# Loading the K cache in 4 MB transfers of 32 KB rows, and stepping attention over pairs of units

## The chip, the cores and the metric

The kernel runs on one core of a Trainium2 chip. The metric is the device time of one execution in microseconds (us), lower being better. A run also has a span, from the first to the last instruction of the profile, which is about 1.9 us shorter. A single-core run is called fast or slow by its distance from the fastest run of the same kernel; where a kernel ran once, its state is unknown. Each profile gives the TensorE clock that was granted (1.00 is full speed).

## The reference

A decode step (one token for each of two batch entries): a layer norm, attention over the last 2048 of 8192 cached positions, and an MLP with a squared ReLU, all added to the input. Everything is bf16.

```python
# B=2, Sq=1, D=576, 32 query heads on 16 K/V heads, Dh=128, window W=2048, F=4608
xn = layernorm(x)
q = xn @ wq                                         # wq: 576 x 4096
k, v = k_cache[:, :, Sk - W:], v_cache[:, :, Sk - W:]   # [2, 16, 2048, 128] each
p = softmax(q k^T * Dh**-0.5)
attn = (p v) @ wo                                   # wo: 4096 x 576
h = relu(xn @ w1 + b1) ** 2                         # w1: 576 x 4608
return x + attn + h @ w2 + b2                       # w2: 4608 x 576
```

Each of K and V has 16.8 MB in the window, the four weight matrices 20 MB together: 53.6 MB to bring in, and very little arithmetic on each byte.

## The kernel before

The work is cut into 8 units, each of four K/V heads of one batch entry. A unit's K (2 MB) lies in SBUF with 128 partitions = 32 chunks of positions x 4 heads, and each partition holds one row of 16 KB (64 positions x 128 x 2 bytes). V lies in the same way.

```python
TH = 4; CP = P // TH            # 4 heads, 32 chunks
NJ = W // CP                    # 64 positions in a row
UE = NJ * Dh                    # 8192 elements, 16 KB
kvpool = ctx.enter_context(tc.tile_pool(name="kvpool", bufs=6))   # 6 slots for K, V and w2

def unit_view(cache, u):
    tq, b = divmod(u, B)
    return cache[b, tq * TH:(tq + 1) * TH, S0:Sk, :].rearrange("h (c j) d -> c h (j d)", c=CP)
```

TensorE transposes K (two bf16 as one f32), ACT and DVE take turns in evicting 128x1024 from PSUM, and eight matmuls make half of a unit's scores. The softmax and the product with V (called PV here) follow one and two units later. `sc_ps`, `pv_ps` and `kT_ps` are the PSUM tiles of these steps.

```python
dst = kT[:, gw * PG:(gw + 1) * PG, :, :].rearrange("p i s e -> p (i s e)")   # contiguous
...
pe_mm(sc_ps[32 * k:32 * (k + 1), :, :], lhsT=qz[...], rhs=kT[:, e, :, 32 * k:32 * (k + 1)], ...)
...
def step(u, p=None, o=None):       # unit u: K transposes and scores; softmax of u-1; PV of p = u-2
    transposes(u, 0); softmax_max(u - 1); transposes(u, 1); softmax_exp(u - 1) ...
# ... (cut) the order of the large transfers on one queue:
# k0 wq k1 v0 w1 k2 v1 k3 v2 k4 v3 k5 v4 k6 v5 wo0 k7 v6 v7 wo1 w2
```

Of the kernel before, what the change touches and what calls it, by code (L numbers as in the profile page):

```python
# [8 lines left out]
F32 = mybir.dt.float32  # L9
# [7 lines left out]
def kernel(  # L17
# [14 lines left out]
    nc = tc.nc  # L32
# [14 lines left out]
    NC = TH * rep  # L47
    NQ = Hkv // TH
    NU = NQ * B
    JG = 8  # L50
    NG = NJ // JG
    NT = NJ // 4
    PG = JG // 2
    GW = NT // PG
    UE = NJ * Dh

    HP = 2 * D // P
# [14 lines left out]
    BIG = 1e30  # L72

    const = ctx.enter_context(tc.tile_pool(name="const", bufs=1))
    kvpool = ctx.enter_context(tc.tile_pool(name="kvpool", bufs=6))
    ktpool = ctx.enter_context(tc.tile_pool(name="ktpool", bufs=2))
    wbig = ctx.enter_context(tc.tile_pool(name="wbig", bufs=1))
    work = ctx.enter_context(tc.tile_pool(name="work", bufs=2))
    keep = ctx.enter_context(tc.tile_pool(name="keep", bufs=3))
# [2 lines left out]
    def pe_mm(out, **kw):  # L82
        return tc.keep_in_program_order(nc.tensor.matmul(out, **kw))  # L83
# [9 lines left out]

    k_tiles, v_tiles, w_tiles, wo_tiles, w2_tiles = {}, {}, {}, {}, {}

    def unit_view(cache, u):
        tq, b = divmod(u, B)
        return cache[b, tq * TH:(tq + 1) * TH, S0:Sk, :].rearrange("h (c j) d -> c h (j d)", c=CP)

    def issue_kv(tiles, cache, u, name, parts=1):  # L100
        tl = kvpool.tile([P, UE], BF16, tag="kv", name=f"{name}_{u}")
        v = unit_view(cache, u)
        n = UE // parts
        tiles[u] = tl
        return [lambda i=i: nc.sync.dma_start(out=tl[:, i * n:(i + 1) * n], in_=v[:, :, i * n:(i + 1) * n])  # L105
                for i in range(parts)]

    def issue_w(wt, name, width):
        tl = wbig.tile([P, HP * FL], BF16, tag="wbig", name=f"{name}_sb")
        nc.sync.dma_start(out=tl[:, 0:HP * width], in_=wt.rearrange("d (s l) -> (d s) l", s=2)  # L110
                          .rearrange("(p r) l -> p (r l)", r=HP))
        w_tiles[name] = tl

    def issue_wo(t):
        if t == 0:
            wo_tiles["all"] = wbig.tile([P, B * WR, D], BF16, tag="wbig", name="wo_sb")
        tl = wo_tiles["all"][:, t * WR:(t + 1) * WR, :]
        n = P * WR
        nc.sync.dma_start(out=tl, in_=A_wo[t * n:(t + 1) * n, :].rearrange("(p r) n -> p r n", r=WR))
        wo_tiles[t] = tl  # L120

    w2_rows = {}

    def issue_w2(g, r0, r1):
        if r0 == 0:
            w2_rows[g] = kvpool.tile([P, FR * D], BF16, tag="kv", name=f"w2_{g}")
        tl = w2_rows[g][:, r0 * D:r1 * D]
        rows = B_w2[g * HW:(g + 1) * HW, :].rearrange("(p r) n -> p (r n)", r=FR)
        nc.sync.dma_start(out=tl, in_=rows[:, r0 * D:r1 * D])
        w2_tiles[(g, r0)] = tl  # L130
# [1 line left out]
    x_sb = const.tile([B + 1, D], BF16, name="x_sb")  # L132
    nc.scalar.dma_start(out=x_sb[0:B, :], in_=x2d)
    b1_sb = const.tile([NG4, HW], BF16, name="b1_sb")
    for g in range(2):
        nc.scalar.dma_start(out=b1_sb[2 * g:2 * g + 2, :], in_=B_b1[2 * g * HW:2 * (g + 1) * HW].rearrange("(g n) -> g n", g=2))
    for i in range(2):
        nc.scalar.dma_start(out=x_sb[B:B + 1, i * OH:(i + 1) * OH],
                            in_=B_b2[i * OH:(i + 1) * OH].rearrange("(o n) -> o n", o=1))
    eps_t = const.tile([B, 1], F32, name="eps_t")  # L140
    nc.vector.memset(eps_t[:], 1e-5)
    warm = const.tile([B, 122], F32, name="warm")
    nc.scalar.activation(out=warm[:, 0:1], in_=eps_t[:], func=ACT.Sqrt)
    for f in issue_kv(k_tiles, A_k_cache, 0, "k"):
        f()
    issue_w(A_wq, "wq", QL)
    ones_f = work.tile([P, P], F32, tag="mix0", name="ones_f")
    nc.vector.memset(ones_f[:], 1.0)
# [118 lines left out]

    kT_tiles, sc_tiles, pT_tiles, acc_tiles, sm_tiles = {}, {}, {}, {}, {}

    def transposes(u, g):  # L270
        k_sb = k_tiles[u]
        w, gw = divmod(g, GW)
        if gw == 0:
            kT_tiles[(u, w)] = ktpool.tile([P, NT, P, 2], BF16, tag="kT_sb", name=f"kT_{u}_{w}")
        kT = kT_tiles[(u, w)]
        kT_ps = psum.tile([P, PG, P], F32, tag="kT", bufs=3, name=f"kT_ps_{u}_{g}")
        for i in range(PG):
            q = g * PG + i
            pe_tr(out=kT_ps[:, i, :], in_=k_sb[:, 2 * q * Dh:2 * (q + 1) * Dh].bitcast(F32),
                                identity=ident_f[:])  # L280
        src = kT_ps[:].rearrange("p i s -> p (i s)").bitcast(BF16)
        dst = kT[:, gw * PG:(gw + 1) * PG, :, :].rearrange("p i s e -> p (i s e)")
        if g % 2 == 0:
            pin(nc.scalar.copy(out=dst, in_=src))  # L284
        else:
            pin(nc.vector.tensor_copy(out=dst, in_=src))  # L286

    def scores(u, w):
        tq, b = divmod(u, B)
        if w == 0:  # L290
            sc_tiles[u] = psum.tile([P, NT, 32], F32, tag="sc", bufs=2, name=f"sc_ps_{u}")
            pe_mm(sc_tiles[u][:].rearrange("p t s -> p (t s)"), lhsT=qhead[:], rhs=khead[:],
                             start=True, stop=False, skip_group_check=True)
        sc_ps = sc_tiles[u]
        kT = kT_tiles.pop((u, w))[:].rearrange("p t s e -> p e t s")
        for e in range(2):
            for k in range(4):
                pe_mm(sc_ps[32 * k:32 * (k + 1), :, :],
                                      lhsT=qz[:, e, b * NQ + tq, w, :, :].rearrange("p j c -> p (j c)"),
                                      rhs=kT[:, e, :, 32 * k:32 * (k + 1)], start=False, stop=(w == 1 and e == 1),  # L300
                                      skip_group_check=True, tile_position=(0, 32 * k))

    sm_cur = {}
# [1 line left out]
    def softmax_max(u):  # L305
        sc_ps = sc_tiles.pop(u)[:].rearrange("p t s -> p (t s)")
        mx = work.tile([P, 1], F32, tag="mx", name=f"mx_{u}")
        pin(nc.vector.tensor_reduce(out=mx[:], in_=sc_ps, axis=AX.X, op=ALU.max))  # L308
        m2 = work.tile([P, NC], F32, tag="m2", name=f"m2_{u}")
        pin(nc.vector.tensor_scalar(out=m2[:], in0=offm[:], scalar1=mx[:, 0:1], scalar2=None, op0=ALU.add))  # L310
        gmax = work.tile([P, NC], F32, tag="gmax", name=f"gmax_{u}")
        nc.gpsimd.partition_all_reduce(gmax[:], m2[:], channels=P, reduce_op=ReduceOp.max)  # L312
        sm_cur[u] = (sc_ps, gmax)
# [20 lines left out]
    def pv_start(u):  # L334
        pv_cur[u] = psum.tile([P, 4, Dh], F32, tag="misc", name=f"pv_ps_{u}")
# [28 lines left out]
    wo_state = {}  # L364

    def pv_out(u):
        tq, b = divmod(u, B)
        t, half = divmod(tq, 2)
        if u % (2 * B) == 0:
            sm_tiles[t] = psum.tile([P, B, Dh + 1], F32, tag="sm", name=f"sm_{t}")  # L370
# [80 lines left out]
                                 rhs=w2_sb[:, o + i * OQ:o + (i + 1) * OQ], start=False, stop=(r == FR - 1),  # L451
                                 skip_group_check=True, tile_position=(0, 32 * i))

    def load_k(u):
        for f in issue_kv(k_tiles, A_k_cache, u, "k"):
            f()

    def load_v(u):
        for f in issue_kv(v_tiles, A_v_cache, u, "v"):
            f()  # L460

    W2P = [(0, 0, 9), (1, 0, 9), (2, 0, 9), (3, 0, 7), (3, 7, 9)]

    load_k(1)
    load_v(0)
    issue_w(B_w1, "w1", FL)
    load_k(2)
    load_v(1)
    load_k(3)

    NR = NT // 4

# [3 lines left out]
            pv(u, i)  # L476
        pv_mix(u)

    def step(u, p=None, o=None):
        if p is not None:  # L480
            pv_start(p)
        transposes(u, 0)
        softmax_max(u - 1)
        transposes(u, 1)
        softmax_exp(u - 1)
        transposes(u, 2)
        if p is not None:
            pv(p, 0)
        transposes(u, 3)
        if p is not None:  # L490
            pv(p, 1)
        softmax_tr(u - 1)
        if o is not None:
            pv_out(o)
        transposes(u, 4)
        scores(u, 0)
        for g in range(GW + 1, NG):
            transposes(u, g)
        for i in range(2, NR):
# [12 lines left out]
    step(1)
    pv_all(0)
    mlp_h_start()
    mlp_h_all()
    mlp_h_end()
    load_k(4)
    for u in range(2, NU - 1):
        step(u, u - 2 if u > 2 else None, u - 3 if u > 2 else None)
        if u == 2:  # L520
            out_acc(res_b[:], lambda a, z: x_sb[:, a:z], start=True)
        if u + 1 < NU - 1:
            load_v(u + 1)
        if u == 4:
            issue_wo(0)
        if u + 3 < NU:
            load_k(u + 3)
        if u == 5:
            load_v(NU - 1)
    issue_wo(1)  # L530
    for w in W2P:
        issue_w2(*w)
    step(NU - 1, NU - 3, NU - 4)
    pv_start(NU - 2)
    for i in range(NR):
        pv(NU - 2, i)
    softmax_max(NU - 1)
    pv_out(NU - 3)
    softmax_exp(NU - 1)
    pv_mix(NU - 2)  # L540
    softmax_tr(NU - 1)
    pv_out(NU - 2)
    pv_all(NU - 1)
    wo_acc(0)
    pv_out(NU - 1)
    mlp_o(*W2P[0])
    wo_acc(1)
# [47 lines left out]
```

## Time and profile before

| | before |
|---|---|
| time | 134.14 us median of 4 runs (133.96 to 134.19) |
| span of the profiled run | 132.2 us, granted clock 0.884 |
| bytes read | 53.62 MB |
| busy of PE, DVE, ACT | 89.0, 59.1, 44.2 us |
| mean packet of 16 KB (2048 of them) | 0.616 us, 426 GB/s over 16 engines |
| idle of the 16 DMA engines, from span start to last packet | 3.0 us, of which 2.1 before the first |

The prediction below shows the main lines of this profile.

 "Packets" here are the trace's records of single DMA moves; on the large loads there is one for each row, and a mean packet time means their mean.

### The profile page before, as it was taken

The numbers are of one execution on the slowest core, as the hardware profiler recorded it, in microseconds if no ns is written. First come the engines' busy times: TensorE is split into PE (matmuls) and PEld (weight loads), VectorE is DVE, ScalarE is ACT, GpSimd is POOL, SyncE is SP. The second block draws the span as 40 slices with busy tenths as digits, with TensorE's granted clock in tenths as the row PEclk, the third lists the DMA queues.
The fourth block names the chain that finished last, engine by engine and source line by source line (L and its number), as shares of the span: only waits on it lengthen the run. The fifth ranks groups of instructions, "written<-read, shape, count | busy, mean of one in ns | idle before, by whom it ended". The sixth has DMA issues, their size and how long they took to land.

```text
span 132.2 us, 2040 instructions
## 1 busy us (share of the span) xinstructions
PE 89.0 (67%) x830; PEld 54.7 (41%) x830; DVE 59.1 (45%) x150; ACT 44.2 (33%) x64; POOL 7.7 (6%) x26
## 2 busy tenths in 40 slices
PE   0069319789862967879889389789303996399761
PEld 0059202639521354744466064466003661155540
DVE  6944400224640019246675823778800358644011
ACT  2705401015700226438457145357100751200011
POOL 7700000001000001000010000010000000000000
PEclk9999995955999599689999977999985699959999
DMA  4999989999998999999999999999999999999950
GB/s 154 389 451 479 413 382 431 431 484 477 439 404 350 436 416 441 426 446 416 431 431 426 436 421 439 426 429 431 428 441 416 446 423 422 429 420 433 419 238 1
DMA packets 3632, 53.74 MB, mean 406 GB/s; under 512 B 412, under 2 KB 420, under 8 KB 680
## 3 DMA queue, kind: packets, MB, share of 16 engines
q1 hardware_dynamic: 3604, 53.61, 95.2%
q8 instruction: 6, 0.10, 0.3%
q10 hardware_dynamic: 20, 0.01, 0.0%
q14 instruction: 2, 0.02, 0.0%
HBM read 53.62 MB, written 0.00 MB: 405 GB/s over the span
## 4 chain that ended last, share of the span: by engine, by line
DMA 72%; PE 20%; DVE 2%; ACT 2%; issue 1%; SPq 1%; DVEq 0%; ACTq 0%
DMA k<-in_A_k_cache_dram 44%; DMA w<-in_B_w_dram 14%; DMA wq_sb<-in_A_wq_dram 13%; PE kT_ps L86 10%; PE sc_ps L83 4%; PE q_ps L83 3%; PE pv_ps L83 2%; PE qs_ps L83 1%; DVE kT L286 1%; ACT kT L284 1%; ACT pr L323 1%; PE sm L83 1%; DVE qrow L250 1%; SPq L105 0%; DVE qz L266 0%
## 5 line engine op out<-in xcount | busy, mean ns | idle before, releaser
L86 PE MATMUL kT_ps<-ident_f,k 128*128 128x128 f32 x256 | 41.4, 319 | 12.6 <-DMA k<-in_A_k_cache_dram 12.1
L284 ACT COPY kT<-kT_ps 128x1024 bf16<-128x1024 bf16 x32 | 31.9, 1011 | 36.8 <-PE kT_ps L86 34.0
L86 PEld LDWEIGHTS kT_ps<-ident_f,k 128*128 128x128 f32 x256 | 34.4, 165 | 21.9 <-issue 16.6
L286 DVE COPY kT<-kT_ps 128x1024 bf16<-128x1024 bf16 x32 | 22.1, 691 | 31.9 <-PE kT_ps L86 31.8
L83 PE MATMUL sc_ps<-kT,qz 128*32 128x512 bf16 x128 | 10.7, 418 | 4.5 <-DVE kT L286 2.8
L83 PE MATMUL pv_ps<-v,pT 128*32 128x512 bf16 x128 | 11.7, 435 | 1.0 <-DVE acc L358 0.8
L312 POOL PARTITION_ALL_REDUCE gmax<-m x8 | 2.9, 365 | 103.1 <-DVE m L310 103.1
L323 ACT ACTIVATE pr<-sc_ps,nb 128x512 bf16<-128x512 f32 x8 | 5.5, 687 | 7.9 <-DVE nb L320 7.9
L83 PEld LDWEIGHTS <-xnT 128*4 128x4 bf16 x90 | 2.9, 105 | 11.6 <-issue 11.0
L308 DVE TENSOR_REDUCE mx<-sc_ps 128x1 f32<-128x512 f32 x8 | 5.5, 683 | 3.1 <-PE sc_ps L83 3.1
L83 PE MATMUL q_ps<-wq_sb,xnT 128*4 128x512 bf16 x36 | 3.7, 592 | 4.5 <-DMA wq_sb<-in_A_wq_dram 4.5
L83 PEld LDWEIGHTS <-qz 128*32 128x32 bf16 x128 | 2.3, 98 | 10.1 <-DVE kT L286 6.3
L83 PE MATMUL h_ps<-w_sb,xnT 128*4 128x384 bf16 x54 | 3.9, 420 | 3.4 <-DMA w_sb<-in_B_w_dram 3.4
L358 DVE SCALAR_TENSOR_TENSOR mix<-pv_ps,own_j,mix 128x128 f32<-128x128 f32 x16 | 5.6, 352 | 0.6
L329 DVE STREAM_TRANSPOSE pT<-pr 128x512 bf16<-128x512 bf16 x8 | 5.6, 702 | 0.2 <-ACT pr L323 0.2
L86 PE MATMUL pro_ps<-ident,xs 2*128 2x2 bf16 x10 | 0.6, 164 | 7.6 <-DVE xs L180 7.6
L83 PE MATMUL out_ps<-wo_sb,ws 128*2 128x288 bf16 x64 | 5.1, 323 | 0.3 <-DVE ws L387 0.3
L83 PEld LDWEIGHTS <-pT 128*32 128x32 bf16 x128 | 2.9, 98 | 5.9 <-issue 3.5
L551 ACT COPY part<-out_ps 2x288 f32<-2x288 f32 x1 | 0.4, 389 | 13.5 <-PE out_ps L83 13.5
L83 PE MATMUL sm<-acc,tohead 128*64 128x129 f32 x16 | 3.7, 313 | 1.8 <-DVE acc L358 1.8
L431 DVE TENSOR_TENSOR hs<-hT_ps,hodd 128x20 f32<-128x20 f32 (+1 forms) x4 | 0.5, 172 | 9.2 <-ACT hodd L428 9.2
L83 PE MATMUL out_ps<-w,hT_sb 128*2 128x288 bf16 x54 | 3.8, 286 | 1.1 <-DMA w<-in_B_w_dram 1.1
(78 smaller groups left out, 58.2 us busy)
## 6 DMA issues: line engine op xcount, KB each, us to landing
k<-in_A_k_cache_dram SPq DMA_DIRECT2D x8, 2048.0 KB, 7.7
v<-in_A_v_cache_dram SPq DMA_DIRECT2D x8, 2048.0 KB, 16.9
w_sb<-in_B_w_dram SPq DMA_DIRECT2D x1, 5184.0 KB, 19.3
wq_sb<-in_A_wq_dram SPq DMA_DIRECT2D x1, 4608.0 KB
wo_sb<-in_A_wo_dram SPq DMA_DIRECT2D x2, 2304.0 KB
w<-in_B_w_dram SPq DMA_DIRECT2D x3, 1296.0 KB, 27.2
w<-in_B_w_dram SPq DMA_DIRECT2D x1, 1008.0 KB
w<-in_B_w_dram SPq DMA_DIRECT2D x1, 288.0 KB
```

What stands on the lines that cost most here:

```text
L83: return tc.keep_in_program_order(nc.tensor.matmul(out, **kw))
L86: return tc.keep_in_program_order(nc.tensor.transpose(**kw))
L250: nc.vector.tensor_copy(out=qrow[:, 0, :], in_=q_ps[0][0:RB, :])
L284: pin(nc.scalar.copy(out=dst, in_=src))
L286: pin(nc.vector.tensor_copy(out=dst, in_=src))
L308: pin(nc.vector.tensor_reduce(out=mx[:], in_=sc_ps, axis=AX.X, op=ALU.max))
L312: nc.gpsimd.partition_all_reduce(gmax[:], m2[:], channels=P, reduce_op=ReduceOp.max)
L323: pin(nc.scalar.activation(out=pr[:], in_=sc_ps, func=ACT.Exp, bias=nb[:], scale=scale, accum_out=acc[:, Dh:Dh + 1]))
L329: pin(nc.vector.transpose(out=pT[:].rearrange("p t m -> p (t m)"), in_=pr[:]))
L358: op = nc.vector.scalar_tensor_tensor(out=nx, in0=pv_ps[:, j, :], scalar=own_j[:, j:j + 1], in1=acc, op0=ALU.mult, op1=ALU.add)
L431: nc.vector.tensor_tensor(out=hs[:].rearrange("p (g r) b -> p r g b", g=NG4)[:, r0:r0 + n, g:g + 2, :], in0=even[:, :, g:g + 2, :], in1=od ...
L551: cp(out=part[:, i * OH:(i + 1) * OH], in_=out_ps[32 * i:32 * i + B, :])
```

## The change

Its intent: half as many K transfers, of rows twice as long. Two units (a pair) share one 4 MB K tile, whose 128 partitions are 16 chunks x 8 heads with 32 KB rows. The transposed K then holds the two units' heads side by side, so evictions write runs of 16 elements and the scores read every second group of four. SBUF for 4 MB tiles is found by giving V three slots, and by putting odd K pairs where wq and w1 had been. So the second K pair now waits for the product with w1, and the loop steps over pairs: 8 slices of transposes for both units, then scores of both, with two softmaxes and two PVs in between.

```diff
-    kvpool = ctx.enter_context(tc.tile_pool(name="kvpool", bufs=6))
+    kvpool = ctx.enter_context(tc.tile_pool(name="kvpool", bufs=3))
+    kpool = ctx.enter_context(tc.tile_pool(name="kpool", bufs=1))
+    wopool = ctx.enter_context(tc.tile_pool(name="wopool", bufs=1))
...
+    def load_k(pr):                      # K2 = 8 heads, C2 = 16 chunks
+        t, b = divmod(pr, B)
+        if pr % 2 == 0:
+            tl = kpool.tile([P, 2 * UE], BF16, tag="kA", name=f"k_{pr}")
+        else:
+            tl = wbig.tile([P, 2 * UE], BF16, tag="wbig", name=f"k_{pr}")
+        nc.sync.dma_start(out=tl[:], in_=A_k_cache[b, t * K2:(t + 1) * K2, S0:Sk, :]
+                          .rearrange("h (c j) d -> c h (j d)", c=C2))
+        k_tiles[pr] = tl
...
-        dst = kT[:, gw * PG:(gw + 1) * PG, :, :].rearrange("p i s e -> p (i s e)")
+        dst = kT[:, gw * PG:(gw + 1) * PG, :, a, :, :].rearrange("p i c h e -> p (i c) (h e)")
...
-                                      rhs=kT[:, e, :, 32 * k:32 * (k + 1)], start=False, stop=(w == 1 and e == 1),
+                                      rhs=kT[:, e, :, nb * k:nb * (k + 1), q * TH:(q + 1) * TH],
...
+    issue_w(B_w1, "w1", FL)
+    load_v(2)
...                                       # softmax, PV of units 0 and 1; the MLP's first product
     mlp_h_end()
-    load_k(4)
-    for u in range(2, NU - 1):
-        step(u, u - 2 if u > 2 else None, u - 3 if u > 2 else None)
...
+    load_k(1)
+    load_v(3)
+    load_k(2)
+    load_v(4)
+    pair(1)
+    load_k(3)
+    pair(2, None, 2, (more_v5, lambda: load_v(6)))
+    pair(3, 3, 4, (lambda: load_v(7), lambda: None), lambda: wo_acc(0))
```

More of the change, by code (lines that the diff above doesn't have):

```diff
@@ L49 @@
     NU = NQ * B
-    JG = 8
-    NG = NJ // JG
+    NP = NU // 2
+    K2 = 2 * TH
+    C2 = P // K2
     NT = NJ // 4
-    PG = JG // 2
+    PG = 4
     GW = NT // PG
+    NG = 4 * GW
     UE = NJ * Dh
@@ L94, with unit, load_v @@
     k_tiles, v_tiles, w_tiles, wo_tiles, w2_tiles = {}, {}, {}, {}, {}
-    def unit_view(cache, u):
-        tq, b = divmod(u, B)
-        return cache[b, tq * TH:(tq + 1) * TH, S0:Sk, :].rearrange("h (c j) d -> c h (j d)", c=CP)
-    def issue_kv(tiles, cache, u, name, parts=1):
-        tl = kvpool.tile([P, UE], BF16, tag="kv", name=f"{name}_{u}")
-        v = unit_view(cache, u)
-        n = UE // parts
-        tiles[u] = tl
-        return [lambda i=i: nc.sync.dma_start(out=tl[:, i * n:(i + 1) * n], in_=v[:, :, i * n:(i + 1) * n])
-                for i in range(parts)]
+    def unit(u):
+        pr, q = divmod(u, 2)
+        t, b = divmod(pr, B)
+        return 2 * t + q, b
+    def load_k(pr):
+        t, b = divmod(pr, B)
+        if pr % 2 == 0:
[5 more added lines that the diff above has]
+        k_tiles[pr] = tl
+    def load_v(u):
+        tq, b = unit(u)
+        tl = kvpool.tile([P, UE], BF16, tag="v", name=f"v_{u}")
+        nc.sync.dma_start(out=tl[:], in_=A_v_cache[b, tq * TH:(tq + 1) * TH, S0:Sk, :]
+                          .rearrange("h (c j) d -> c h (j d)", c=CP))
+        v_tiles[u] = tl
     def issue_w(wt, name, width):
@@ L114, in issue_wo @@
     def issue_wo(t):
-        if t == 0:
-            wo_tiles["all"] = wbig.tile([P, B * WR, D], BF16, tag="wbig", name="wo_sb")
-        tl = wo_tiles["all"][:, t * WR:(t + 1) * WR, :]
+        tl = wopool.tile([P, WR, D], BF16, tag="wo_sb", name=f"wo_{t}")
         n = P * WR
-        nc.sync.dma_start(out=tl, in_=A_wo[t * n:(t + 1) * n, :].rearrange("(p r) n -> p r n", r=WR))
+        nc.sync.dma_start(out=tl[:], in_=A_wo[t * n:(t + 1) * n, :].rearrange("(p r) n -> p r n", r=WR))
         wo_tiles[t] = tl
@@ L124, in issue_w2 @@
     def issue_w2(g, r0, r1):
-        if r0 == 0:
-            w2_rows[g] = kvpool.tile([P, FR * D], BF16, tag="kv", name=f"w2_{g}")
-        tl = w2_rows[g][:, r0 * D:r1 * D]
+        if g == 0:
+            w2_rows["all"] = kpool.tile([P, (NG4 - 1) * FR * D], BF16, tag="kA", name="w2_rows")
+        if g == NG4 - 1 and r0 == 0:
+            w2_rows[g] = kvpool.tile([P, FR * D], BF16, tag="v", name=f"w2_{g}")
+        o = g * FR * D
+        tl = w2_rows["all"][:, o:o + FR * D] if g < NG4 - 1 else w2_rows[g][:, r0 * D:r1 * D]
         rows = B_w2[g * HW:(g + 1) * HW, :].rearrange("(p r) n -> p (r n)", r=FR)
@@ L134 @@
     b1_sb = const.tile([NG4, HW], BF16, name="b1_sb")
-    for g in range(2):
-        nc.scalar.dma_start(out=b1_sb[2 * g:2 * g + 2, :], in_=B_b1[2 * g * HW:2 * (g + 1) * HW].rearrange("(g n) -> g n", g=2))
-    for i in range(2):
-        nc.scalar.dma_start(out=x_sb[B:B + 1, i * OH:(i + 1) * OH],
-                            in_=B_b2[i * OH:(i + 1) * OH].rearrange("(o n) -> o n", o=1))
     eps_t = const.tile([B, 1], F32, name="eps_t")
@@ L143 @@
     nc.scalar.activation(out=warm[:, 0:1], in_=eps_t[:], func=ACT.Sqrt)
-    for f in issue_kv(k_tiles, A_k_cache, 0, "k"):
-        f()
+    load_k(0)
     issue_w(A_wq, "wq", QL)
@@ L268, with transposes @@
     kT_tiles, sc_tiles, pT_tiles, acc_tiles, sm_tiles = {}, {}, {}, {}, {}
-    def transposes(u, g):
-        k_sb = k_tiles[u]
-        w, gw = divmod(g, GW)
-        if gw == 0:
-            kT_tiles[(u, w)] = ktpool.tile([P, NT, P, 2], BF16, tag="kT_sb", name=f"kT_{u}_{w}")
-        kT = kT_tiles[(u, w)]
-        kT_ps = psum.tile([P, PG, P], F32, tag="kT", bufs=3, name=f"kT_ps_{u}_{g}")
+    def transposes(pr, g):
+        k_sb = k_tiles[pr]
+        w, gw = divmod(g, 2 * GW)
+        a, gw = divmod(gw, GW)
+        if a == 0 and gw == 0:
+            kT_tiles[(pr, w)] = ktpool.tile([P, NT, C2, 2, K2, 2], BF16, tag="kT_sb", name=f"kT_{pr}_{w}")
+        kT = kT_tiles[(pr, w)]
+        kT_ps = psum.tile([P, PG, P], F32, tag="kT", bufs=3, name=f"kT_ps_{pr}_{g}")
         for i in range(PG):
-            q = g * PG + i
+            q = (a * 2 + w) * NT + gw * PG + i
             pe_tr(out=kT_ps[:, i, :], in_=k_sb[:, 2 * q * Dh:2 * (q + 1) * Dh].bitcast(F32),
                                 identity=ident_f[:])
-        src = kT_ps[:].rearrange("p i s -> p (i s)").bitcast(BF16)
-        dst = kT[:, gw * PG:(gw + 1) * PG, :, :].rearrange("p i s e -> p (i s e)")
+        src = kT_ps[:].rearrange("p i s -> p (i s)").bitcast(BF16).rearrange("p (n x) -> p n x", x=2 * K2)
+        dst = kT[:, gw * PG:(gw + 1) * PG, :, a, :, :].rearrange("p i c h e -> p (i c) (h e)")
         if g % 2 == 0:
@@ L288, in scores @@
     def scores(u, w):
-        tq, b = divmod(u, B)
+        tq, b = unit(u)
+        pr, q = divmod(u, 2)
         if w == 0:
@@ L294, in scores @@
         sc_ps = sc_tiles[u]
-        kT = kT_tiles.pop((u, w))[:].rearrange("p t s e -> p e t s")
+        kT = kT_tiles[(pr, w)][:].rearrange("p t c a h e -> p e t (c a) h")
+        nb = 32 // TH
         for e in range(2):
             for k in range(4):
-                pe_mm(sc_ps[32 * k:32 * (k + 1), :, :],
+                pe_mm(sc_ps[32 * k:32 * (k + 1), :, :].rearrange("m t (n h) -> m t n h", h=TH),
                                       lhsT=qz[:, e, b * NQ + tq, w, :, :].rearrange("p j c -> p (j c)"),
-                                      rhs=kT[:, e, :, 32 * k:32 * (k + 1)], start=False, stop=(w == 1 and e == 1),
+                                      rhs=kT[:, e, :, nb * k:nb * (k + 1), q * TH:(q + 1) * TH],
+                                      start=False, stop=(w == 1 and e == 1),
                                       skip_group_check=True, tile_position=(0, 32 * k))
@@ L366, in pv_out @@
     def pv_out(u):
-        tq, b = divmod(u, B)
+        tq, b = unit(u)
         t, half = divmod(tq, 2)
@@ L452, in mlp_tail @@
                                  skip_group_check=True, tile_position=(0, 32 * i))
-    def load_k(u):
-        for f in issue_kv(k_tiles, A_k_cache, u, "k"):
-            f()
-    def load_v(u):
-        for f in issue_kv(v_tiles, A_v_cache, u, "v"):
-            f()
     W2P = [(0, 0, 9), (1, 0, 9), (2, 0, 9), (3, 0, 7), (3, 7, 9)]
-    load_k(1)
     load_v(0)
-    issue_w(B_w1, "w1", FL)
-    load_k(2)
     load_v(1)
-    load_k(3)
     NR = NT // 4
@@ L477, in pv_all, with pair @@
         pv_mix(u)
-    def step(u, p=None, o=None):
-        if p is not None:
-            pv_start(p)
-        transposes(u, 0)
-        softmax_max(u - 1)
-        transposes(u, 1)
-        softmax_exp(u - 1)
-        transposes(u, 2)
-        if p is not None:
-            pv(p, 0)
-        transposes(u, 3)
-        if p is not None:
-            pv(p, 1)
-        softmax_tr(u - 1)
-        if o is not None:
-            pv_out(o)
-        transposes(u, 4)
-        scores(u, 0)
-        for g in range(GW + 1, NG):
-            transposes(u, g)
-        for i in range(2, NR):
-            if p is not None:
-                pv(p, i)
-        if p is not None:
-            pv_mix(p)
-        scores(u, 1)
+    def pair(pr, o=None, p0=None, after=(), mid=None):
+        p1 = p0 + 1 if p0 is not None else None
+        u0, u1 = 2 * pr, 2 * pr + 1
+        if p0 is not None:
+            pv_start(p0)
+        for g in range(2 * GW):
+            transposes(pr, g)
+            if p0 is None:
+                continue
+            if g == 0:
+                softmax_max(p0)
+            if g == 1:
+                softmax_exp(p0)
+            if g == 2:
+                softmax_max(p1)
+            if g == 3:
+                softmax_tr(p0)
+                softmax_exp(p1)
+                if o is not None:
+                    pv_out(o)
+            if g == 5:
+                softmax_tr(p1)
+                pv(p0, 0)
+                pv(p0, 1)
+        if p0 is not None:
+            pv(p0, 2)
+        scores(u0, 0)
+        if p0 is not None:
+            pv(p0, 3)
+            pv_mix(p0)
+            after[0]()
+        scores(u1, 0)
+        if mid is not None:
+            mid()
+        for g in range(2 * GW, NG):
+            transposes(pr, g)
+            if p0 is None:
+                continue
+            if g == 2 * GW + 1:
+                pv_out(p0)
+                pv_start(p1)
+                pv(p1, 0)
+            if g == 2 * GW + 4:
+                pv(p1, 1)
+        if p0 is not None:
+            pv(p1, 2)
+            pv(p1, 3)
+            pv_mix(p1)
+            after[1]()
+        scores(u0, 1)
+        scores(u1, 1)
     for g in range(NG):
@@ L508 @@
     q_all()
-    for w in range(2):
-        scores(0, w)
-    load_v(2)
-    step(1)
+    issue_w(B_w1, "w1", FL)
+    load_v(2)
+    b1_sb = const.tile([NG4, HW], BF16, name="b1_sb")
+    nc.gpsimd.dma_start(out=b1_sb[:], in_=B_b1.rearrange("(g n) -> g n", g=NG4))
+    nc.gpsimd.dma_start(out=x_sb[B:B + 1, :], in_=B_b2.rearrange("(o n) -> o n", o=1))
+    for w in range(2):
+        for u in range(2):
+            scores(u, w)
+    for u in range(2):
+        softmax_max(u)
+        softmax_exp(u)
+        softmax_tr(u)
     pv_all(0)
+    pv_out(0)
+    pv_all(1)
     mlp_h_start()
@@ L516, with more_v5 @@
     mlp_h_end()
-    load_k(4)
-    for u in range(2, NU - 1):
-        step(u, u - 2 if u > 2 else None, u - 3 if u > 2 else None)
-        if u == 2:
-            out_acc(res_b[:], lambda a, z: x_sb[:, a:z], start=True)
-        if u + 1 < NU - 1:
-            load_v(u + 1)
-        if u == 4:
-            issue_wo(0)
-        if u + 3 < NU:
-            load_k(u + 3)
-        if u == 5:
-            load_v(NU - 1)
+    pv_out(1)
+    load_k(1)
[3 more added lines that the diff above has]
+    pair(1)
+    out_acc(res_b[:], lambda a, z: x_sb[:, a:z], start=True)
+    load_k(3)
+    def more_v5():
+        load_v(5)
+        issue_wo(0)
+    pair(2, None, 2, (more_v5, lambda: load_v(6)))
+    pair(3, 3, 4, (lambda: load_v(7), lambda: None), lambda: wo_acc(0))
     issue_wo(1)
@@ L532 @@
         issue_w2(*w)
-    step(NU - 1, NU - 3, NU - 4)
     pv_start(NU - 2)
+    softmax_max(NU - 2)
+    softmax_max(NU - 1)
+    pv_out(NU - 3)
+    softmax_exp(NU - 2)
+    softmax_tr(NU - 2)
     for i in range(NR):
         pv(NU - 2, i)
-    softmax_max(NU - 1)
-    pv_out(NU - 3)
     softmax_exp(NU - 1)
+    softmax_tr(NU - 1)
     pv_mix(NU - 2)
-    softmax_tr(NU - 1)
     pv_out(NU - 2)
     pv_all(NU - 1)
-    wo_acc(0)
     pv_out(NU - 1)
```

## The prediction

116.6 us to the last scores, 22.9 of tail and 1.9 beyond the span come to its 141.5 us. What went is an argument that longer rows have little to win, the reason for keeping 691 ns for the new eviction (so it stands as an assumption; 690 was measured), and the third rival, slower evictions or scores, whose size rested on a figure not shown. The "cold start" stands on the trace: 12 transposes took 2.79 us after 7.54 us idle, with a granted clock of 0.50 from 101 to 104 us, and 1.50 us after 0.76, with 1.00 from 66 to 69.

> **What bounds the kernel now.** I read the page of the profile first: the slices of the span, the DMA queues, and the shares of the chain that ended last.
>
> ```profile
> DMA  4999989999998999999999999999999999999950
> q1 hardware_dynamic: 3604, 53.61, 95.2%
> DMA 72%; PE 20%; DVE 2%; ACT 2%; issue 1%; SPq 1%; DVEq 0%; ACTq 0%
> ```
>
> The DMA row is busy in nearly every slice, the main queue's packets fill 95.2% of 16 engines' span, and 72% of the chain is DMA. So the kernel waits for bytes: 53.61 MB / (0.952 x 132.2 us) = 426 GB/s while the engines work. The packet records of the trace show the first large packet at 2.1 us, the last one ending at 128.65 us, and under 0.5 us of idle engine time between 4 and 126 us. The program then needs 3.6 us more. Nothing of the stream's middle can be won by better overlap.
>
> Next I asked the table of engine busy time by stage, because a reordering of transfers moves work between stages (columns: stretch, length, busy of PE, weight loads, DVE, ACT, POOL, clock, DMA share, GB/s).
>
> ```profile
> 24.00:53.00 29.00, 21.34 (x187) 13.92 (x187) 10.28 (x28) 9.10 (x17) 0.73 (x2) 0.82 1.01 431
> 53.00:66.00 13.00, 11.49 (x97) 7.01 (x96) 6.80 (x15) 6.85 (x9) 0.36 (x1) 0.87 1.00 429
> 66.00:101.00 35.00, 23.05 (x201) 13.45 (x201) 19.88 (x47) 14.06 (x18) 1.46 (x4) 0.91 1.01 431
> ```
>
> TensorE is far from idle: it works in every stage, with one 2 MB K slice per unit arriving steadily, and it has only modest slack. That slack is what the change spends. The TensorE timeline gives the cost of one unit (columns: start, duration, engine, line, operation, idle before).
>
> ```profile
> 66.58 1.50 PE L86 MATMUL kT_ps<-ident_f,k 128*128 128x128 f32 x12 [0.76 <-DMA k<-in_A_k_cache_dram]
> ...
> 73.40 0.62 PE L83 MATMUL sc_ps<-kT,qz 128*32 128x512 bf16 x8 [0.24 <-DVE kT L286]
> ...
> 101.43 2.79 PE L86 MATMUL kT_ps<-ident_f,k 128*128 128x128 f32 x12 [7.54 <-DMA k<-in_A_k_cache_dram]
> ```
>
> A full unit (32 transposes, their evictions, scores, softmax of the previous unit, PV of an earlier one) takes 66.58 to 74.0 = 7.4 us. The transfers of a unit (K and V, 2 x 4.93 us) take 9.9 us. Unit 5 starts at its K's landing; the last unit starts at 101.43, and after its scores (110.4) the program needs 21.8 us more. The evictions that pace the transposes are:
>
> ```profile
> L284 ACT COPY kT<-kT_ps 128x1024 bf16<-128x1024 bf16 x32 | 31.9, 1011 | 36.8 <-PE kT_ps L86 34.0
> L286 DVE COPY kT<-kT_ps 128x1024 bf16<-128x1024 bf16 x32 | 22.1, 691 | 31.9 <-PE kT_ps L86 31.8
> ```
>
> [...] 12 transposes took 2.79 us after 7.54 us idle and 1.50 us after 0.76. [...] I keep 691 ns.
>
> **The change part by part.**
>
> *Longer K rows.* Mean packet times by row size in the trace: 0.616 us for 16 KB, 0.686 for 18,432 bytes, 1.365 for 36,864, 1.542 for 41,472. That is 426 to 432 GB/s. A 32 KB row should take 1.22 us instead of 2 x 0.616 = 1.23. Each engine carries 32 such rows: about 0.4 us saved in all. No byte is removed.
>
> *Order of the transfers.* Before, the queue ran k0, wq, k1, v0, w1, k2, v1, k3, v2, k4. After, the order of instructions on the issuing queue is k0 (4 MB), wq, v0, v1, w1, v2, v3, then k1 (4 MB), k2, v4, k3, v5, wo0, v6, v7, wo1, w2. Pair 1 (units 2 and 3) can't start before k1 lands. In units of 8 packets per engine: k0 9.73 + wq 10.92 + v0, v1 9.86 + w1 12.34 + v2, v3 9.86 + k1 9.73 = 62.4 us. Added to the start at 2.1 us this gives 64.5. The same sum for the fifth K before gives 64.8, against a first transpose at 66.58, so I add 1.7: pair 1 starts at about 66.3 us.
>
> This is the point of the prediction. Before, at 66.6 us TensorE had finished units 0 to 4 and had three to go. After, at 66.3 it has done units 0 and 1 and has six to go, having stood idle since w1's product (about 46 to 53 us). The transfers left then last only 60 us.
>
> *TensorE's work after 66.3 us.* Pair 1 carries no PV: 16 groups at about 0.6 us (1.0 us of ACT and 0.69 of DVE alternate over three PSUM buffers) and four scores of 0.55 to 0.85, waits for the last eviction included: 13.0 us, plus 1.5 us for its cold start. Pair 2 carries PV of two units and two softmaxes: 2 x 7.4 = 14.8 plus 2 us, because both exponentials and both probability transposes stand between its first eight evictions: 16.9. Pair 3 the same plus one output projection of 2.0 (32 matmuls, 121.62 to 123.58 before): 18.9. Sum: 66.3 + 1.5 + 13.0 + 16.9 + 18.9 = 116.6 for the end of the last scores, against 110.4 before.
>
> *The tail.* Now the softmax of both last units comes after the last scores. First PV of the tail: rest of the mixes 0.7, two maxima of 0.92, 0.4 for the bias, exponential 0.95, transpose 0.75, some waits: 5 us (0.8 before). Then 4 us to the second PV (111.22 to 115.06 before), 4.8 us for it, its mixes, the first w2 part and the normalisation, 2.0 + 2.4 for the second projection and two w2 parts, 2.5 for part, tail and cast, 2.1 to the end of the span: 22.9 us with rounding. Span 116.6 + 22.9 = 139.5. The profiled run before took 134.06 for a span of 132.2, so I add 1.9: **141.5 us**.
>
> *Buffers.* Three V slots: v5 waits for PV of unit 2 and v7 for PV of unit 4, each in the middle of a pair. v7 is due at about 105 on the queue and its slot comes free at about 107: a gap of 2 to 3 us in the stream, perhaps 1 us at v5 or k3. Last w2 landing then 130 to 132 us, still ahead of TensorE's use, so the gap is not added.
>
> **The rivals.** (1) *Stream still the bound*: if pairs run as fast as pure TensorE time (10.5 + 13.6 + 15.6 instead of 48.8 us), the last scores end at 107 and the stream decides: 134.2 - 0.4 plus 0 to 2 us of slot gaps, 134 to 136 us. For it: DMA busy at 95%. Against it: evictions and softmax already held a unit to 7.4 us, with 6.8 of TensorE work. (2) *Gain*: even with the stream perfect and the tail kept, the floor is 2.1 + 125.2 + 3.6 + 1.9 = 132.8 us, 1% faster. Over 2% faster would need a DMA rate that no row size here shows. [...]
>
> **Range and chances.** TensorE's chain is summed over 70 us with 10% doubt on waits and clock: 137.5 to 146.5. Under 2% change needs rival 1. Faster 0.02, same 0.12, slower 0.86.
>
> **What would show it.** First transposes of pair 1 at 66 us with over 10 us of TensorE idle before, waiting for K; then no more K waits: k2 and k3 landed before TensorE asks. Chain with much less DMA, far more PE, DVE and ACT. Evictions near 1011 and 691 ns; K packets near 1.22 us. Last scores at 114 to 119 us. A wait of the queue for PV before v7, with a dip in the DMA row. If pair 1 starts well before 66 us, or pairs take under 12, 15 and 17 us, I am wrong.

## More of the kernel before

```profile
GB/s 154 389 451 479 413 382 431 431 484 477 439 404 350 436 416 441 426 446 416 431 431 426 436 421 439 426 429 431 428 441 416 446 423 422 429 420 433 419 238 1
...
k<-in_A_k_cache_dram SPq DMA_DIRECT2D x8, 2048.0 KB, 7.7
```

The rate lies near 430 GB/s whatever large load is in flight: by their mean packets, 426 to 432 GB/s for rows of 10,368 to 41,472 bytes.

## The result

The changed kernel takes **180.96 us** (median of 4 runs; 178.69 and 178.84 in the fast, 183.08 and 183.96 in the slow). The ratio to before is 1.333, 95% interval 1.330 to 1.336. A ratio is the mean time of one kernel's fast runs over that of the other's of the same rounds, so it is not quite the ratio of the medians quoted. The prediction had the direction right and the size wrong: 141.5 us, range 137.5 to 146.5.

The profiled run after (span 177.0 us, clock 0.774) in the same views. First its page: the DMA row and the rate in 40 slices, the main queue (packets, MB, share of 16 engines), the chain that ended last, the evictions (count | busy, mean ns | idle before), and K's transfers.

```profile
DMA  7899999899999999999899979999899999999930
GB/s 186 170 239 237 235 416 400 370 441 414 450 452 411 433 370 230 237 215 192 185 237 237 215 218 370 244 222 207 170 218 426 405 437 437 428 413 433 418 123 1
...
q1 hardware_dynamic: 3028, 53.61, 94.7%
...
DMA 58%; PE 27%; DVE 9%; ACT 3%; issue 1%; ACTq 0%; DVEq 0%
...
L294 ACT COPY kT<-kT_ps 128x1024 bf16<-128x1024 bf16 x32 | 31.7, 1012 | 78.5 <-PE kT_ps L90 78.5
L296 DVE COPY kT<-kT_ps 128x1024 bf16<-128x1024 bf16 x32 | 22.1, 690 | 75.3 <-PE kT_ps L90 75.3
...
k<-in_A_k_cache_dram SPq DMA_DIRECT2D x4, 4096.0 KB, 32.5
```

By the DMA row and the queue's share of 94.7% (95.2% before), the engines are as busy as before, although the kernel is a third slower and moves the same 53.61 MB. **Busy is not moving.** The rate row shows it: 170 to 244 GB/s in slices 1 to 5, 16 to 24 and 26 to 30 (counted from 1), and 370 to 452 in the others until the stream ends. The table by stage takes three stretches (stretch, length, busy of PE, weight loads, DVE, ACT, POOL, granted clock, DMA share, GB/s): by the order of the queue, the first and third hold K alone, the second w1 and V.

```profile
2.00:22.00 20.00, 0.57 (x10) 0.41 (x10) 5.83 (x22) 3.85 (x6) 4.54 (x14) 1.00 1.05 232
36.00:55.00 19.00, 10.44 (x86) 4.18 (x86) 6.49 (x18) 3.73 (x8) 0.73 (x2) 0.58 1.01 431
66.00:88.00 22.00, 0.00 (x0) 0.00 (x0) 0.00 (x0) 0.00 (x0) 0.00 (x0) 0.50 1.03 216
```

From 66 to 88 us no compute engine does anything, and the DMA share is full at half the rate. In the packet records, 512 rows of 32 KB took a mean of **2.448 us** (median 2.51), which is 214 GB/s over 16 engines; before, a 16 KB row took 0.616. All other sizes are nearly as they were: means of 0.687 for 18,432 bytes, 1.410 for 36,864 and 1.538 for 41,472, and a median of 0.611 us for V's 16 KB (mean 0.657; 0.616 before). So the change made the loads of K, and only these, run at half their rate. TensorE's timeline shows what it paid (start, duration, instructions, idle before and its releaser):

```profile
88.59 6.26 PE L90 MATMUL kT_ps<-ident_f,k 128*128 128x128 f32 x32 [23.38 <-DMA k<-in_A_k_cache_dram]
...
107.55 3.90 PE L90 MATMUL kT_ps<-ident_f,k 128*128 128x128 f32 x20 [3.76 <-DMA k<-in_A_k_cache_dram]
...
134.35 3.65 PE L90 MATMUL kT_ps<-ident_f,k 128*128 128x128 f32 x16 [10.19 <-DMA k<-in_A_k_cache_dram]
```

All three remaining pairs wait for their K, where the prediction had one such wait, for pair 1 alone at 66.3 us.

### The profile page after: what moved, and what is told of

The parts are those of the page before. It is cut to its first block, busy times and chain, and to the rows that moved or that the text cites. A ratio compares the mean times of both kernels' runs of the same rounds, so it can differ in the third digit from the quotient of the medians.

```text
span 177.0 us, 2015 instructions
## 1 busy us (share of the span) xinstructions
PE 92.5 (52%) x830; PEld 57.3 (32%) x830; DVE 59.3 (33%) x150; ACT 47.0 (27%) x66; POOL 8.9 (5%) x28
## 3 DMA queue, kind: packets, MB, share of 16 engines
q1 hardware_dynamic: 3028, 53.61, 94.7%
## 4 chain that ended last, share of the span: by engine, by line
DMA 58%; PE 27%; DVE 9%; ACT 3%; issue 1%; ACTq 0%; DVEq 0%
DMA k<-in_A_k_cache_dram 46%; PE kT_ps L90 13%; DMA w_sb<-in_B_w_dram 12%; PE out_ps L87 5%; PE h_ps L87 3%; ACT kT L294 2%; DVE kT L296 2%; PE sc_ps L87 2%; PE pv_ps L87 2%; DVE pT L342 2%; DVE mix L371 1%; PE q_ps L87 1%; DVE mx L321 1%; PE sm L87 1%; ACT pr L336 1%
## 5 line engine op out<-in xcount | busy, mean ns | idle before, releaser
L90 PEld LDWEIGHTS kT_ps<-ident_f,k 128*128 128x128 f32 x256 | 35.8, 169 | 60.5 <-issue 40.8
L294 ACT COPY kT<-kT_ps 128x1024 bf16<-128x1024 bf16 x32 | 31.7, 1012 | 78.5 <-PE kT_ps L90 78.5
L87 PE MATMUL pv_ps<-v,pT 128*32 128x512 bf16 x128 | 12.4, 475 | 7.2 <-DVE pT L342 4.0
L325 POOL PARTITION_ALL_REDUCE gmax<-m x8 | 2.9, 366 | 146.5 <-DVE m L323 146.0
L87 PE MATMUL sm<-acc,tohead 128*64 128x129 f32 x16 | 4.4, 369 | 7.3 <-DVE acc L371 7.3
L87 PEld LDWEIGHTS sm<-acc,tohead 128*64 128x64 f32 x16 | 1.9, 171 | 10.9 <-issue 10.1
L368 DVE TENSOR_SCALAR mix<-pv_ps,own_j 128x128 f32<-128x128 f32 x8 | 2.7, 338 | 7.8 <-PE pv_ps L87 7.8
L87 PE MATMUL h_ps<-w_sb,xnT 128*4 128x384 bf16 x54 | 5.0, 521 | 0.1
L87 PE MATMUL out_ps<-wo,ws 128*2 128x288 bf16 x64 | 4.8, 307 | 0.0
L87 PE MATMUL out_ps<-w_rows,hT_sb 128*2 128x288 bf16 x54 | 4.7, 338 | 0.0
## 6 DMA issues: line engine op xcount, KB each, us to landing
w<-in_B_w_dram SPq DMA_DIRECT2D x1, 1008.0 KB, 18.9
```

The source lines that it names most:

```text
L87: return tc.keep_in_program_order(nc.tensor.matmul(out, **kw))
L90: return tc.keep_in_program_order(nc.tensor.transpose(**kw))
L294: pin(nc.scalar.copy(out=dst, in_=src))
L325: nc.gpsimd.partition_all_reduce(gmax[:], m2[:], channels=P, reduce_op=ReduceOp.max)
L368: op = nc.vector.tensor_scalar(out=nx, in0=pv_ps[:, j, :], scalar1=own_j[:, j:j + 1], scalar2=None, op0=ALU.mult)
```

## The experiments

Four theories were open. *Length* (A): rows of 32 KB are slow in themselves. *Memory* (B): the memory side is slow, with eight heads read at once, each at a distance of 2 MB. *Form* (C): the transfer is slow because its source of 16 chunks x 8 rows is spread over the DMA engines, or over the partitions, in some bad way. *Order*: K's rate is only a part, and the new order of steps costs much too. Thirteen kernels ran. Those that read K at another place, or put it into another order, are called wrong. The comparison with the reference for these inputs does not notice which part of K was read, so that it proves nothing there, and little about K in the kernels marked correct. Runs of the kernel before, made beside them, took 134.04 to 134.59 us. For each, the table by stage shows the same stretch, 3 to 11 us, in which only the first K loads.

### k16_32x4: the change with K as before

Each pair's K is loaded as two 2 MB transfers of 16 KB rows, with 4 heads x 32 chunks; the transposed K is laid out for each unit on its own. Order, pools and pairs stay changed. 3 rounds, correct.

```diff
-        nc.sync.dma_start(out=tl[:], in_=A_k_cache[b, t * K2:(t + 1) * K2, S0:Sk, :]
-                          .rearrange("h (c j) d -> c h (j d)", c=C2))
+        for q in range(2):
+            h = (2 * t + q) * TH
+            nc.sync.dma_start(out=tl[:, q * UE:(q + 1) * UE], in_=A_k_cache[b, h:h + TH, S0:Sk, :]
+                              .rearrange("h (c j) d -> c h (j d)", c=CP))
```

> The changed kernel with its queue order, slots and pairs, but each 4 MB of K loaded as two transfers of 16 KB rows from 4 heads by 32 chunks, as before; correct result. All three theories of the slow K (A: rows of 32 KB are slow in themselves; B: eight heads 2 MB apart collide in HBM; C: the 16 by 8 shape [...]) expect K packets of 0.62 us here. The prediction's own chain of TensorE work after the late second K pair then expects 141.5 us (137.5 to 146.5), and the slow K costs the rest, about 37 us. If the order costs nothing: 134 us.

138.98 us (137.58 to 139.21), ratio to before 1.033 (1.028 to 1.038). The mean 16 KB packet is back at 0.625 us. Its table by stage, and its chain:

```profile
3.00:11.00 8.00, 3.25 (x23) 3.09 (x24) 5.60 (x19) 3.87 (x5) 3.53 (x12) 1.00 1.00 421
```

```profile
PE 46%; DMA 26%; DVE 15%; ACT 6%; issue 2%; SPq 1%; POOL 1%; ACTq 0%; DVEq 0%
```

The whole rest of the change, with K in its old form, costs 3.3%. The other 40 us are in how K is loaded, so the order explains only the small rest. The chain is what the prediction described: DMA no longer bounds the kernel, TensorE and DVE do.

### k16_16x8: the new mapping in rows of 16 KB

The mapping of 8 heads x 16 chunks stays; each 32 KB row is loaded in two halves by two transfers. Correct.

```diff
+        v = A_k_cache[b, t * K2:(t + 1) * K2, S0:Sk, :].rearrange("h (c j) d -> c h (j d)", c=C2)
+        for i in range(2):
+            nc.sync.dma_start(out=tl[:, i * UE:(i + 1) * UE], in_=v[:, :, i * UE:(i + 1) * UE])
```

> The changed kernel with each 4 MB K transfer cut into its two column halves: rows of 16 KB, still 8 heads by 16 chunks, same partitions, correct result. A (row length): packets of 0.62 us and about 141 us. B (heads) and C (shape): 16 KB packets of about 1.25 us, about 178 us.

178.6 us, as slow as the change. The 256 packets of the first K, of 16 KB each, took a median of 1.23 us (mean 1.19), where 0.611 was the median before. The table by stage:

```profile
3.00:11.00 8.00, 0.58 (x10) 0.41 (x10) 4.93 (x18) 2.86 (x4) 3.52 (x12) 1.00 1.04 226
```

Short rows are slow as well, so A falls.

### k32_plain: 32 KB rows from a plain source

The same 128 rows of 32 KB, but from a source with one row dimension and a pitch of 34 KB. Wrong.

```diff
+        src = A_k_cache
+        nc.sync.dma_start(out=tl[:], in_=bass.AP(src.tensor, src.offset + pr * 64 * Dh,
+                                                 [[136 * Dh, P], [1, 2 * UE]]))
```

> The changed kernel with K rows of 32 KB read from 128 rows of one pitch of 34 KB (one dimension of 128 in the source, no heads; wrong result on purpose). A: packets of 2.5 us, about 178 us. B and C: packets of about 1.22 us, about 141 us.

141.38 us. The 32 KB packets have a median of 1.213 us and a mean of 1.267. The table by stage:

```profile
3.00:11.00 8.00, 0.58 (x10) 0.42 (x10) 4.93 (x18) 2.86 (x4) 3.52 (x12) 1.00 0.93 399
```

A is dead: 32 KB rows can run at full rate, and gain nothing over 16 KB rows either (2 x 0.611 is 1.222). This kernel is the predicted one, with the one rate restored that went wrong, and it is used as such below. Its span is 139.6 us; the prediction's sum was 139.5. What memory or form explains is the difference to the changed kernel: 178.8 - 141.4 = **37.4 us**.

### k32_16x8_odd and k32_32x4_alias: the form or the memory side

The first keeps the form of 16 x 8 and drops the heads: all rows from one region, with pitches of 34 and 274 KB. The second keeps the heads and drops the form: 32 heads at their distance of 2 MB, four rows of each. Both wrong on purpose, one look each.

```diff
+    # k32_16x8_odd
+    [[1096 * Dh, C2], [136 * Dh, K2], [1, 2 * UE]]
+    # k32_32x4_alias
+    [[Sk * Dh, 32], [2 * UE, 4], [1, 2 * UE]]
```

> The changed kernel with K rows of 32 KB in 16 by 8 shape, but from addresses with odd pitches (34 KB inner, 274 KB outer) and no heads (wrong result on purpose). A and C: packets of 2.5 us, about 178 us. B: 1.22 us, about 141 us.

> The changed kernel with K rows of 32 KB in 32 by 4 shape, the outer step 2 MB (all 32 heads of both batches, 4 chunks of each; wrong result on purpose): the strongest case for heads that collide in memory. B (heads): 2.5 us a packet or more, 178 us or more. C (shape): about 1.22 us a packet, about 141 us.

180.37 us against 142.15; median packets 2.548 against 1.213 us. Tables by stage, first k32_16x8_odd, then k32_32x4_alias:

```profile
3.00:11.00 8.00, 0.58 (x10) 0.41 (x10) 4.92 (x18) 2.87 (x4) 3.52 (x12) 1.00 0.99 205
```

```profile
3.00:11.00 8.00, 0.58 (x10) 0.41 (x10) 4.93 (x18) 2.86 (x4) 3.52 (x12) 1.00 1.00 419
```

Without heads the slowness stays, and with 32 of them at 2 MB it is gone. B falls on both sides, and the form is left.

### k32_64x2: is any two-dimensional source but 16 x 8 fine?

The source is 64 x 2 rows, with pitches of 70 and 34 KB. Wrong on purpose, one look.

```diff
+    [[280 * Dh, 64], [136 * Dh, 2], [1, 2 * UE]]
```

> The changed kernel with K rows of 32 KB at odd pitches in 64 by 2 shape (wrong result on purpose). [...] If every two-dimensional source but 32 by 4 [...]: 2.5 us a packet, about 178 us. If an outer dimension of more than 16 [...]: 1.22 us, about 141 us.

141.77 us, median packet 1.213 us. The table by stage:

```profile
3.00:11.00 8.00, 0.57 (x10) 0.41 (x10) 4.94 (x18) 2.86 (x4) 3.53 (x12) 1.00 0.90 386
```

So 128 x 1, 64 x 2 and 32 x 4 run at full rate, and 16 x 8 at half. Why was not shown: the trace does not say which engine carries which row.

### k32_two64 and k32_plain64: only half of the partitions at a time

A guess to be tested: if the form matters through the partitions that are written at one time, a transfer that reaches only 64 partitions should be slow too. k32_two64 splits the changed kernel's transfer into four heads to partitions 0 to 63 and four to 64 to 127; k32_plain64 does so with the plain source. Both wrong on purpose (the first by the order of its rows), one look each.

```diff
+    # k32_two64
+        v = A_k_cache[b, t * K2:(t + 1) * K2, S0:Sk, :].rearrange("h (c j) d -> c h (j d)", c=C2)
+        for i in range(2):
+            nc.sync.dma_start(out=tl[i * 64:(i + 1) * 64, :], in_=v[:, i * TH:(i + 1) * TH, :])
+    # k32_plain64
+        src, at = A_k_cache, A_k_cache.offset + pr * 64 * Dh
+        for i in range(2):
+            nc.sync.dma_start(out=tl[i * 64:(i + 1) * 64, :],
+                              in_=bass.AP(src.tensor, at + i * 64 * 136 * Dh, [[136 * Dh, 64], [1, 2 * UE]]))
```

> The changed kernel with each 4 MB of K as two transfers of 16 by 4 rows of 32 KB, to partitions 0 to 63 and 64 to 127 (partition order differs, wrong result on purpose). [...] 2.5 us a packet and about 178 us[...]. If only eight rows per engine were the trouble: 1.22 us, about 141 us.

> As k32_plain (rows of 32 KB, one pitch of 34 KB, wrong result on purpose), but in two transfers of 64 rows, to partitions 0 to 63 and 64 to 127. If the SBUF partitions written at one time decide [...]: 2.5 us a packet, about 178 us, although the source has one dimension only. If the two-dimensional source with an outer 16 is what is slow: 1.22 us, about 141 us.

180.29 and 182.67 us; mean packets 2.480 and 2.535 us, which is 211 and 207 GB/s over 16 engines. The table by stage of k32_plain64:

```profile
3.00:11.00 8.00, 0.58 (x10) 0.42 (x10) 4.95 (x18) 2.87 (x4) 3.54 (x12) 1.00 0.96 197
```

k32_plain64 moves the same rows to the same partitions as k32_plain; only the cut into two transfers differs, and it is slow. So the source's two dimensions are not needed for the slow rate: transfers to 64 partitions have it too (197 GB/s in this stretch, where k32_plain has 399). Nor is it enough to have two transfers: k16_32x4 loads K in two to 128 partitions each, at 421. That fits the guess, and does not show by what mechanism.

### k32_16x7 and k32_plain112: 112 partitions

The last test of how many partitions a transfer reaches: 112 (16 x 7, or plain), with the other 16 loaded apart. The expectation of the first was a mixture, of fast packets for the most part. Both wrong.

```diff
+        nc.sync.dma_start(out=tl[0:112, :], in_=bass.AP(src.tensor, at, [[1096 * Dh, 16], [136 * Dh, 7], [1, 2 * UE]]))
+        # k32_plain112: [[136 * Dh, 112], [1, 2 * UE]]
+        for i in range(2):
+            nc.sync.dma_start(out=tl[112:P, i * UE:(i + 1) * UE],
+                              in_=bass.AP(src.tensor, at + i * UE, [[1096 * Dh, 16], [1, UE]]))
```

> The changed kernel with K rows of 32 KB at odd pitches in 16 by 7 shape (partitions 0 to 111; the last 16 rows in two transfers of 16 KB rows; wrong result on purpose). [...] If a 16-row outer dimension is slow [...]: 2.5 us for all 112.

> As k32_16x7 (112 rows to partitions 0 to 111, the rest apart), but from a source with one pitch of 34 KB. If the 2.18 us a packet of k32_16x7 came from its 112 partitions: about 2.2 us again, about 179 us. If it came from the two-dimensional source: 1.22 to 1.4 us, about 145 us.

179.5 and 180.72 us. Median 2.240 and 2.214 us for a 32 KB packet, and nine in ten of them between 1.5 and 2.9 us. k32_16x7 is a **miss**: neither the mixture nor the 2.5 us that had been expected of it. k32_plain112 shows that the value belongs to the 112 partitions and not to the two-dimensional source. Why 112 partitions take so long stays open. The 16 partitions loaded apart are not the reason: the first rounds of the first K, before those are loaded, already take 1.6 to 2.3 us on the mean.

### before_k16x8: the form alone, in the kernel before

The kernel before, whole, with K's source read as 8 heads x 16 chunks (16 KB rows, 2 MB transfers). Wrong. Two runs (194.89 and 197.45).

```diff
+        if name == "k":
+            tq, bb = divmod(u, B)
+            h0 = tq // 2 * 2 * TH
+            v = cache[bb, h0:h0 + 2 * TH, S0 + tq % 2 * (W // 2):S0 + (tq % 2 + 1) * (W // 2), :].rearrange(
+                "h (c j) d -> c h (j d)", c=16)
```

> The kernel before with nothing but the K transfers reshaped: 2 MB each, 16 KB rows, but from 8 heads by 16 chunks (wrong result on purpose). If the shape alone makes K slow (C): 16 KB packets of 1.2 us, 16.8 MB of K take about 39 us longer, about 173 us. If the slow K needs the new order or the 4 MB size: 134 us.

196.17 us, ratio 1.461. The shape of the transfer alone spoils the kernel before, with no pair, pool or order touched. It cost more than expected: 62 us instead of the 39 or so. The table by stage, once for the first K and once near the end:

```profile
3.00:11.00 8.00, 0.58 (x10) 0.41 (x10) 4.93 (x18) 2.89 (x5) 2.38 (x10) 1.00 1.07 231
...
166.00:190.00 24.00, 19.24 (x251) 10.43 (x251) 10.30 (x26) 4.68 (x8) 0.36 (x1) 0.92 0.46 183
```

The last stretch runs with the DMA engines under half busy: by the packet records only one to three moves are in flight at a time from 176 to 186 us. The engines' idle time makes up about 11 us of the surplus (14.4 us in all against 3.0 before). V's packets between the slow K loads also grew (means of 0.68 to 0.89 us): over K and V together the mean is 0.98 us, where half of 0.616 and half of 1.22 would be 0.92. With 2048 such packets, or 128 on each engine, this is 128 x 0.06 = 8 us. Why the stream ends so unevenly was not tested.

### k16_last_by_unit: what the pairs cost

k16_32x4 with its last pair stepped unit by unit: unit 6's transposes, scores and softmax come before unit 7's, as in the kernel before. 3 rounds, correct.

```diff
-    pair(3, 3, 4, (lambda: load_v(7), lambda: None), lambda: wo_acc(0))
+    last_pair(3)        # for unit 6, then unit 7: 8 groups of transposes, scores; softmax of 6 inside 7
```

> K16_32x4 with the last pair worked unit by unit, so that the softmax of unit 6 runs beside the transposes of unit 7 and only one softmax stands after the last scores; correct result. If the remaining 4.7 us over the kernel before is mostly the tail with its two softmaxes (25.6 us after the last scores against 21.8): about 4 us less than k16_32x4, 134.5 to 136.5 us. If it is the late second K pair: 138 to 139.5 us.

136.2 us (135.45 to 137.13), ratio 1.017 (1.013 to 1.022): 2.4 us faster than k16_32x4 by the means, 2.8 by the medians. About 4 had been expected. Its chain, and then the line of its timeline and that of k16_32x4 with the first PV after the last scores:

```profile
DMA 53%; PE 28%; DVE 7%; ACT 5%; SPq 2%; issue 2%; POOL 1%; ACTq 0%; DVEq 0%
```

```profile
112.51 1.05 PE L87 MATMUL pv_ps<-v,pT 128*32 128x512 bf16 x16 [0.80 <-DVE acc L372]
```

```profile
116.20 1.86 PE L87 MATMUL pv_ps<-v,pT 128*32 128x512 bf16 x16 [3.19 <-DVE gs L332]
```

With pairs, the first PV of the tail waits 3.19 us for a softmax that begins only after the last scores. By units it waits 0.80, and the stream is the bound again.

### k16_early: the second K pair early

k16_32x4 with pair 1 loaded ahead of w1 (pairs 0 to 2 in one buffer) and the MLP's first product after pair 1; one small PSUM tile of the MLP also moved to another slot. 3 rounds, correct.

```diff
-        if pr % 2 == 0:
+        if pr < NP - 1:
...
     for g in range(NG):
         transposes(0, g)
+    load_k(1)
     q_all()
...
+    pair(1)
     mlp_h_start()
     mlp_h_all()
     mlp_h_end()
-    load_k(1)
+    load_k(2)
```

> K16_32x4 (16 KB rows in 32 by 4 shape, three V slots, pairs) with the second K pair loaded right behind V of units 0 and 1 and worked before w1's product, pairs 1 and 2 in the first pair's buffer; correct result. If the late second K pair is what the order costs (the prediction's step): TensorE starts pair 1 at about 43 us instead of 62.6, the stream ends the kernel again, and 133.5 to 136 us are measured. If stepping over pairs with both last softmaxes in the tail is what costs: 137 to 140 us, as k16_32x4.

144.42 us (143.09 to 145.52; one of four slow), ratio 1.072: a **miss**, it got slower. The issuing queue's timeline and the table by stage, of the profiled run (a slow one, 145.52 us), tell why:

```profile
64.64 1.18 SPq L113 DMA_DIRECT2D k<-in_A_k_cache_dram  x2
```

```profile
60.00:67.00 7.00, 6.38 (x67) 4.08 (x67) 2.77 (x4) 3.95 (x4) 0.00 (x0) 1.00 0.18 54
```

K of pair 2 can be issued only when pair 1's transposes have emptied the one buffer, at 64.64 us. The stream stands still until then, 5.8 us in the bins from 60 to 68 us (54 GB/s in the stretch shown). The clock in this stretch was full, so the slow state does not make this wait, but no fast run has a profile. A 4 MB tile needs a second free 4 MB tile to be loaded ahead, and this kernel has none. With these buffers the early order was not to be had.

## Why the prediction was wrong, and where it was right

**The step that failed is "*Longer K rows*".** It said: "A 32 KB row should take 1.22 us". The row took 2.448. With 32 rows on each engine that is 32 x (2.448 - 1.22) = 39 us more in the stream, and the result is 178.8 - 141.5 = 37 us over the prediction. The step took times from rows of other lengths, all of them of loads from sources of 128 x 1 or 32 x 4 rows. It looked at the row's length, which is harmless (k32_plain: median 1.213), and not at the changed outer dimension, from 32 x 4 to 16 x 8, which is what the runs show to cost it (k32_16x8_odd, k16_16x8, before_k16x8). It named no rival in which the rate of K itself could fall: rivals 1 and 2 took the stream as given, and the third lay on the compute side.

**The mechanism, as far as shown.** Shown: for rows of 32 KB, 16 x 8 to 128 partitions ran at half rate (2.448 us a packet on the mean, 214 GB/s), and so did both transfers to 64 partitions (211 and 207 GB/s); 128 x 1, 64 x 2 and 32 x 4 to 128 partitions ran at full (a median of 1.213 us, 432 GB/s). Not shown: which engine writes which partition, for the trace does not name them, and so by what mechanism the form sets the rate. The records of the first K hold one more trait. In the changed kernel, after a first round of 2.11, the rounds of 16 packets take 2.50 to 2.52 us each, with the fifth at 2.38. The other slow runs have such a dip too: k32_plain64 and k32_two64 in the fifth round (2.38, 2.34), k16_16x8 in the fifth, ninth and thirteenth (1.12, 1.16, 1.15); k32_plain has none. The account that the author gave of these dips was an inference that no run shows, and it is left out; so the cause of the dips, as that of the 2.240 and 2.214 us with 112 partitions, stays open.

**The other steps, tested by k32_plain.** It has the changed kernel's structure and the predicted row time, so it is the run that the other steps of the prediction speak of. Its timeline begins pair 1 with this line:

```profile
66.63 5.88 PE L90 MATMUL kT_ps<-ident_f,k 128*128 128x128 f32 x32 [11.26 <-DMA k<-in_A_k_cache_dram]
```

| step | predicted | k32_plain | changed kernel |
|---|---|---|---|
| pair 1 begins (us) | 66.3 | 66.6 | 88.6 |
| pair 1, 2, 3 take | 14.5, 16.9, 18.9 | 14.8, 15.7, 18.2 | begin 88.6, 107.6, 134.4 |
| last scores end | 116.6 | 115.3 | 153.4 |
| tail | 22.9 | 24.3 | 23.6 |
| span | 139.5 | 139.6 | 177.0 |

- *Order of the transfers*: right in the wait. TensorE stands idle for 11.26 us (predicted: over 10) and begins pair 1 at 66.6 us. In the changed kernel the same sum with the real row time of k0 and k1 (2 x 19.6 us in place of 2 x 9.73) gives 86.0; 88.6 was seen. One reading is wrong: at 66.58 us the kernel before began its fifth unit, so TensorE had finished units 0 to 3 and had four to go, not three. The sum does not use that count.
- *TensorE's work after 66.3 us*: right to 1.3 us, with pairs 2 and 3 a little faster than predicted. "k2 and k3 landed before TensorE asks" holds there, and failed in the changed kernel, with waits of 3.76 and 10.19 us, because K was slow.
- *The evictions*: right. 1012 and 690 ns, against 1011 and 691; the runs of 16 elements cost nothing.
- *The tail*: right in kind, 1.4 us too short. That the predicted span meets k32_plain's to 0.1 us is luck: this error and the 1.3 us of TensorE's work cancel.
- *Buffers*: the slots did hold up the queue (3 V slots: it waited 10.7 us for one PV in k32_plain). The gap in the stream was smaller than feared: 0.3 us near v7, 0.9 near 80 us, 0.3 at 92.

The changed kernel's 178.8 - 134.1 = 44.7 us divide like this, by differences of whole kernels: 37.4 for the form of K's transfers (to k32_plain); 2.4 for K arriving in one 4 MB piece instead of two halves, whose transposes begin at 62.6 and 67.5 us (to k16_32x4, in which the layout of the transposed K differs too); about 2.6 for two softmaxes at the end (to k16_last_by_unit); and about 2 left over, perhaps the late second pair, which no run isolates. The first two differences rest on one run of k32_plain and have some tenths to one us of doubt. No version tried beats the kernel before, and by the prediction's own floor (132.8 us, from 53.6 MB at the measured rate) none with these bytes and this tail could do so by much.

## What to carry to other kernels

When a load's layout changes, check the rate of *that load* in the first run, in GB/s: the DMA engines' busy share stayed at 95% while the bytes came at half speed. Of the sources tried for a transfer to 128 partitions, 128 x 1, 64 x 2 and 32 x 4 rows ran at full rate (432 GB/s by their median packets of 32 KB); 16 x 8 halved it (214 GB/s by the mean), and so did splitting the transfer into partitions 0 to 63 and 64 to 127 (211 and 207). Longer rows gave nothing beyond 16 KB here (1.213 us for 32 KB against 2 x 0.611), while one large tile in place of two costs the time at which the first half could have been used, and needs a second large buffer before it can be loaded ahead.
